# The closing feed-forward block of a cached decode kernel: seven batches moved beside the last tasks, the eighth handled alone

## The chip, the cores and the metric

The kernel runs on one core of a Trainium2 chip. The metric is device microseconds of one execution; the kernel before takes 1171.39 us (median of three runs, 1169.83 to 1171.56). Engines: PE (TensorE, matmuls, with PEld for its weight loads), DVE (VectorE), ACT (ScalarE), POOL (GpSimd), SP (SyncE, which here issues the DMAs).

## The reference

```
x = x + attn(layernorm(x), k_cache, v_cache, wq, wo)      # A
x = x + silu(layernorm(x) @ w1) @ w2                      # B
x = x + attn(layernorm(x), k_cache, v_cache, wq, wo)      # A again, same caches
x = x + silu(layernorm(x) @ w1) @ w2                      # B again
```

`x` is 8 batches x 1 token x 512. `attn` has 32 query heads over 8 KV groups of 8192 keys with 128 elements each, softmax over the keys, and no new key or value. The caches are 8 x 8 x 8192 x 128, bfloat16, K and V. w1 is 512 x 1792, w2 1792 x 512. The layer norm is (x - mean) / sqrt(var + 1e-5), without weights.

## The kernel before, in words

**Tasks.** One task is one (layer, batch, KV group); there are 128, in an order that `make_tasks` makes so that part of the K cache (20 of the 32 granules of a batch: groups 3 to 7) stays in SBUF between layer 0 and layer 1 of a batch. The last eight tasks are batch 7 in layer 1: groups 3 to 7 with kept K (tasks 120 to 124, only V is loaded), then groups 0 to 2 (tasks 125 to 127, K and V loaded). A task is eight positions `p` of the main loop, 1024 keys each.

**Loads.** `ARENA` is 28 slots of 512 KB. `plan_loads` fixes ahead which load goes to which slot, and after which position it may be issued (`after`); SP issues them in that fixed order (`issue_until`, `dma`, L428). Slot 8 is the home of group 3's first kept granule; from task 120 on it is free for other loads.

**One position.** At `p` PE transposes the K block of p + 1 (L523), DVE or ACT evicts it (L531, L529); on odd p PE makes the scores of two blocks (L562); on even p PE does P times V for the two blocks 12 positions back (L628). Between lie the softmax steps of the task before, at fixed phases of p: maximum (L573 to L577), shift (L581, L583), exponential (L587), sum (L593, L595), transposes of P (L603, L607), reciprocal (L614). `emit_norm` (L645) scales a finished head group into `QA`. All engines run their instructions in program order, so a piece that one of them waits for holds back what stands behind it on that engine.

**Pieces beside the tasks.** The end of a layer of a batch is cut in pieces; the main loop emits at most one or two of them per position: for layer 0 `chain_of` (wo, residual, layer norm, w1, Silu, w2, and the next queries, the `asks`). For layer 1, `heads[8]` collects the finished groups of batch 7, and `add_heads(8)` adds, for all eight batches at once, one group's part of the wo product to the PSUM bank `MISC` (`wo_part`, L743, 16 matmuls with 8 columns). The last of these comes after the last task.

**The closing block** (`closing`, L767 to L784) follows when all tasks are done, for eight batches together: residual (L755), layer norm in two passes (`normed`: sum over partitions on POOL, L670 and L672, center L676, square L700, second sum), w1 meanwhile (56 matmuls, L724, each column repeated four times, `AGAIN`), six filler matmuls (`keep_busy(AFTER)`, L543), the inverse root by a seed and three Newton rounds of three DVE instructions (`inverse_root`, L653 to L664), scaling on DVE (`scaled`, L706), Silu on ACT (L780), w2 (56 matmuls, L767) on top of the residual, a copy (L784) and four stores (L962).

Of the kernel before, what the change touches and what calls it, by code (L numbers as in the profile page):

```python
# [33 lines left out]
QSOON = 3  # L34
ASKS = (2, 5)
# [10 lines left out]
AGAIN = 4  # L46
BEFORE, AFTER = 4, 6
# [148 lines left out]
def plan_loads(tasks, kept, nslot, ngran):  # L196

    at = {t: i for i, t in enumerate(tasks)}
    homes = make_homes(kept, nslot, ngran)
# [89 lines left out]
def _build(ctx, nc, A_x, A_k_cache, A_v_cache, A_wq, A_wo, B_w1, B_w2, out):  # L289
# [99 lines left out]
    hsB = PTb[:, 0:FT * B]  # L389
    hB = Pf[:, 0:FT * B]  # L390
    ehB = Pf[:, FT * B:2 * FT * B]
    assert 5 * KT * B <= CPB * NQ * USED and FT * B <= 4 * KT * B and 4 * FT * B <= KB
# [49 lines left out]

    k_slot = {}
# [12 lines left out]
    with nc.Block() as block:  # L456

        @block.sync
        def _(sync_eng):
# [231 lines left out]
            def normed(xv, rx, w_sb, rw, outs, again=1):  # L691

                total(xv, rx, B)
                center(xbB, ["PT", "xb"], xv, rx, B)
                for f in project(w_sb, rw, outs, KT, lambda k: xbB[:, k, :], "xb", B, again=again):
                    f()
                if again > 1:
                    keep_busy(AFTER)
# [6 lines left out]
            def scaled(dst, rdst, n, again=1):  # L705
                op(dve, lambda: dve.tensor_tensor(  # L706
                    dst, MISC[:, 0:n * B * again].rearrange("p (h b) -> p h b", b=B * again)[:, :, 0:B],
                    yr[:, 0:B].unsqueeze(1).to_broadcast([128, n, B]), ALU.mult),
                   reads=["MISC", "yr"], writes=rdst)

            def project(w_sb, rw, outs, kparts, rhs_of, r_rhs, n, parts=1, again=1):

                steps = []
                w = CW if n == 1 else n * again

                def moved(k):
                    if n == 1:
                        return rhs_of(k).to_broadcast([128, w])
                    return rhs_of(k).unsqueeze(1).to_broadcast([128, again, n]) if again > 1 else rhs_of(k)

                for i, o in enumerate(outs):
                    for k in range(kparts):
                        steps.append(
                            lambda i=i, o=o, k=k: pe.matmul(  # L724
                                MISC[:, i * n:i * n + w] if again == 1 else
                                MISC[:, i * w:(i + 1) * w].rearrange("p (r b) -> p r b", b=n),
                                w_sb[:, k, o * 128:(o + 1) * 128], moved(k),
# [33 lines left out]
            def closing(x0, x1, r0, r1):  # L761

                rows = SCp[0]

                def quads(lhs_of, rhs_of, parts, first, last):
                    return [
                        lambda k=k, c=c: pe.matmul(  # L767
                            rows[c * QUAD:c * QUAD + B, 0:128], lhs_of(k, c), rhs_of(k, c),
                            start=first, stop=last and k == parts - 1,
                        )  # L770
                        for k in range(parts) for c in range(KT)
                    ]
# [7 lines left out]
                op(act, lambda: act.activation(hsB, hB, ACT.Silu), reads=["P"], writes=["hsB"])  # L780
# [83 lines left out]
            def add_heads(b):  # L864
# [6 lines left out]
                else:  # L871
                    wo_part(g, lambda h: QAv[:, h, :], every, B, first, last)
# [17 lines left out]
            scaled(QAv, every, HQ)  # L890
# [10 lines left out]
            ntask = len(tasks)  # L901

            for p in range(NG + LP + GPT + 1):
# [49 lines left out]
            assert not queue and not chain and not asks  # L953
# [39 lines left out]
```

## Time and profile before

| | us |
|---|---|
| median of three runs | 1171.39 (1169.83 to 1171.56) |
| the profiled execution | 1173.08 |
| its span | 1171.3 |
| PE busy / DVE / ACT / POOL over the span | 967.9 / 598.1 / 383.0 / 117.6 |
| DMA moved | 467.97 MB, mean 400 GB/s |
| last matmul of wo ends | 1162.3 |
| Silu of the closing block starts | 1167.37 |
| first store issued | 1169.05 |

The profile is of one execution. Times in the trace are microseconds from the start of its span; the execution's own time is 1.8 us longer than the span. "Busy" of PE is that of pipelined matmuls, so it overstates how much of PE is used. A name such as L523 is the line of the kernel that issues the instruction; "a<-b" says which tile is written from which.

### The profile page before, as it was taken

The page shows a single profiled execution, that of the slowest core. Times are in us where ns is not written, and L with a number is a line of the kernel's source. Part 1 is how long each engine was busy: PE and PEld are TensorE (multiplying, and loading weights), DVE is VectorE, ACT ScalarE, POOL GpSimd, SP SyncE. Part 2 cuts the span into 40 slices and gives each one's busy share as a digit, 9 for nine tenths or more (in the row PEclk, how much of TensorE's full clock was granted, in tenths as well). Part 3 has the DMA queues.
Part 4 walks back from the last instruction along what each step waited for, and adds up shares of the span by engine and source line. Part 5 has one row for each costly group of instructions (what it writes and reads, how often), then busy time and mean ns, then how long its engine had stood idle before and what let it go on. Part 6 is the DMA issues. An engine that isn't in the chain of part 4 may idle for free.

```text
span 1171.3 us, 44902 instructions
## 1 busy us (share of the span) xinstructions
PE 967.9 (83%) x19896; PEld 755.5 (65%) x19898; DVE 598.1 (51%) x1932; ACT 383.0 (33%) x660; POOL 117.6 (10%) x300
## 2 busy tenths in 40 slices
PE   4479888898889887888778887899878888788887
PEld 4367765677657675667557765677556666676665
DVE  2235654455545563556544563556445654556544
ACT  1124331343223331343223431334224332343222
POOL 0000111000100111001110111001100111001110
PEclk8789999899989999999998999999999999999999
DMA  9999999999999999999999999999999999999995
GB/s 346 394 398 389 402 408 417 422 397 382 411 423 412 366 409 416 423 395 405 411 423 376 401 408 419 421 383 409 413 421 414 385 408 421 409 387 407 411 411 227
DMA packets 96529, 467.97 MB, mean 400 GB/s; under 512 B 10056, under 2 KB 15952, under 8 KB 72784
## 3 DMA queue, kind: packets, MB, share of 16 engines
q1 hardware_dynamic: 96304, 465.10, 98.7%
q8 instruction: 157, 2.57, 0.9%
q14 instruction: 36, 0.29, 0.1%
q10 hardware_dynamic: 32, 0.00, 0.0%
HBM read 465.05 MB, written 0.01 MB: 397 GB/s over the span
## 4 chain that ended last, share of the span: by engine, by line
DMA 56%; PE 32%; DVE 5%; issue 4%; ACT 2%; SPq 1%; POOL 1%; POOLq 0%; ACTq 0%; DVEq 0%
DMA arena<-in_A_v_cache_dram 29%; DMA arena<-in_A_k_cache_dram 27%; PE TPp L523 11%; PE OTp L628 8%; PE SCp L562 6%; PE MISC L724 3%; ACT P L587 2%; PE TPp L603 2%; DVE arena L531 2%; DVE small L573 2%; PE MISC L743 1%; SPq L428 1%; POOL small L577 1%; DVE small L575 0%; DVE PT L607 0%
## 5 line engine op out<-in xcount | busy, mean ns | idle before, releaser
L523 PE MATMUL TPp<-ident,arena 128*128 128x128 bf16 x5632 | 447.3, 224 | 85.2 <-DMA arena<-in_A_k_cache_dram 82.3
L531 DVE COPY arena<-TPp 128x1024 bf16<-128x1024 bf16 x440 | 303.8, 690 | 327.0 <-PE TPp L523 325.2
L523 PEld LDWEIGHTS TPp<-ident,arena 128*128 128x128 bf16 x5632 | 333.4, 100 | 151.3 <-DMA arena<-in_A_k_cache_dram 99.0
L628 PE MATMUL OTp<-PT,arena 128*128 128x64 bf16 (+1 forms) x8192 | 318.9, 191 | 62.5 <-DMA arena<-in_A_v_cache_dram 39.0
L529 ACT COPY arena<-TPp 128x1024 bf16<-128x1024 bf16 x264 | 266.9, 1011 | 311.3 <-PE TPp L523 311.1
L628 PEld LDWEIGHTS OTp<-PT,arena 128*128 128x128 bf16 x8192 | 274.2, 98 | 104.8 <-DMA arena<-in_A_v_cache_dram 55.5
L562 PE MATMUL SCp<-arena,QB 128*32 128x512 bf16 x2048 | 208.9, 398 | 9.0 <-DVE small L614 4.3
L587 ACT ACTIVATE P<-SCp,small 128x512 bf16<-128x512 f32 x128 | 87.9, 687 | 391.6 <-DVE small L583 204.1
L577 POOL PARTITION_ALL_REDUCE small<-small x128 | 47.5, 371 | 720.4 <-DVE small L575 691.2
L573 DVE TENSOR_REDUCE small<-SCp 128x1 f32<-128x512 f32 x128 | 87.6, 684 | 40.2 <-PE SCp L562 39.2
L562 PEld LDWEIGHTS SCp<-arena,QB 128*32 128x32 bf16 x2048 | 54.0, 93 | 56.1 <-ACT QB L554 6.1
L595 POOL PARTITION_ALL_REDUCE small<-small x128 | 55.9, 436 | 240.7 <-DVE small L593 240.7
L607 DVE COPY PT<-TPp 128x256 bf16<-128x256 bf16 x128 | 37.3, 292 | 74.6 <-PE TPp L603 74.6
L603 PE MATMUL TPp<-ident,P 128*128 128x128 bf16 x512 | 51.2, 223 | 24.9 <-ACT P L587 24.9
L603 PEld LDWEIGHTS TPp<-ident,P 128*128 128x128 bf16 x512 | 29.1, 98 | 57.6 <-ACT P L587 47.0
L593 DVE TENSOR_SCALAR small<-small 128x4 f32<-128x4 f32 x128 | 29.2, 228 | 31.2 <-ACT P L587 29.9
L724 PE MATMUL MISC<-XT,wq 128*128 128x32 bf16 x1024 | 39.8, 177 | 1.5 <-issue 1.5
L724 PEld LDWEIGHTS MISC<-XT,wq 128*128 128x128 bf16 x1024 | 32.2, 96 | 9.0 <-issue 9.0
L743 PE MATMUL MISC<-at,wo 128*128 128x32 bf16 x1024 | 36.0, 176 | 1.4 <-issue 1.4
L743 PEld LDWEIGHTS MISC<-at,wo 128*128 128x128 bf16 x1024 | 31.6, 96 | 5.0 <-issue 5.0
L575 DVE SCALAR_TENSOR_TENSOR small<-small 128x4 f32<-128x4 f32 x128 | 28.5, 223 | 4.5
L581 DVE SCALAR_TENSOR_TENSOR small<-small 128x4 f32<-128x4 f32 x128 | 19.9, 156 | 20.4 <-POOL small L577 20.4
(69 smaller groups left out, 320.1 us busy)
## 6 DMA issues: line engine op xcount, KB each, us to landing
arena<-in_A_v_cache_dram SPq DMA_DIRECT2D x132, 1024.0 KB, 11.3
arena<-in_A_v_cache_dram SPq DMA_DIRECT2D x248, 512.0 KB, 8.0
arena<-in_A_k_cache_dram SPq DMA_DIRECT2D x192, 512.0 KB, 8.0
arena<-in_A_k_cache_dram SPq DMA_DIRECT2D x32, 2048.0 KB, 14.3
arena<-in_A_k_cache_dram SPq DMA_DIRECT2D x16, 1024.0 KB, 11.7
wq<-in_A_wq_dram SPq DMA_DIRECT2D x1, 4096.0 KB, 17.0
wo<-in_A_wo_dram SPq DMA_DIRECT2D x1, 4096.0 KB, 30.1
w<-in_B_w_dram SPq DMA_DIRECT2D x2, 1792.0 KB, 24.9
```

Source lines behind the costliest of these rows:

```text
L523: lambda c=c: pe.transpose(tpv[:, c, :], chunk(slot, h * GRP + c), ident[:, :])
L529: op(act, lambda: act.copy(dst, TPp[tb][:, :]), reads=[f"TP{tb}"], writes=[r_half(slot, h)])
L531: op(dve, lambda: dve.tensor_copy(dst, TPp[tb][:, :]), reads=[f"TP{tb}"], writes=[r_half(slot, h)])
L562: lambda c=c: pe.matmul(SCp[bank][c * QUAD:(c + 1) * QUAD, :], QB[qn][:, NGRAN - 1 - k:NGRAN - 1 - k + QUAD], ARENA[:, slot * SLOT + c * K ...
L573: op(dve, lambda: dve.tensor_reduce(rowmax, SCp[bank][:, :], AX.X, ALU.max), reads=[f"SC{bank}"], writes=["rowmax"])
L577: op(pool, lambda: pool.partition_all_reduce(tops, top, 128, bass.bass_isa.ReduceOp.max), reads=["top"], writes=["tops"])
L587: op(act, lambda: act.activation(P[:, :], SCp[bank][:, :], ACT.Exp, bias=shift, scale=SM_SCALE, accum_out=rs[st]), reads=[f"SC{bank}", "sh ...
L595: op(pool, lambda: pool.partition_all_reduce(ssa[st], ssm[st], 128, bass.bass_isa.ReduceOp.add), reads=[f"ssm{st}"], writes=[f"ssa{st}"])
L603: lambda c=c: pe.transpose(tpv[:, c, :], P[:, c * 128:(c + 1) * 128], ident[:, :])
L628: lambda c=c, cc=cc: pe.matmul(otp, chunk(slot, h * GRP + c), pv[:, cc % CPB, cc // CPB % NQ, k, :].unsqueeze(2).to_broadcast([128, REP, w ...
L724: lambda i=i, o=o, k=k: pe.matmul(MISC[:, i * n:i * n + w] if again == 1 else MISC[:, i * w:(i + 1) * w].rearrange("p (r b) -> p r b", b=n ...
L743: lambda o=o, h=h: pe.matmul(MISC[:, o * w:(o + 1) * w], wo_sb[:, h, o * 128:(o + 1) * 128], rhs_of(h).to_broadcast([128, w]) if n == 1 el ...
```

## The change

The closing block is split. Batches 0 to 6 are closed by `close_rest`, 18 pieces that the main loop emits from p = 979, when the last of their tasks is done: the first four on every odd position (`CLOSES` of the others wait), the other 14 one per position from p = 1000, the start of task 125. They work in slot 8, which the planner now keeps free from task 120 on. Their Silu is made of Exp, an addition, a reciprocal and a product. Batch 7 alone adds its heads to `MISC` afterwards, from p = 1014 on (one column, repeated 32 times), and `close_last` follows the last task: sums of x and of x squared come out of two DVE instructions and go through POOL together; the shift by the mean is on ACT; w1 and w2 work with one column; variance and inverse root are 12 DVE instructions, with Newton rounds of two; Silu reads `MISC` and has the inverse root as its scale. The filler matmuls are two before w1 and one behind it. The four stores become eight: seven rows each early, one row each at the end.

```
+CLOSES = 14
...
-AGAIN = 4
-BEFORE, AFTER = 4, 6
+BEFORE, BETWEEN, AFTER = 4, 2, 1
...
+    closes = at[(1, nb - 1, min(homes))]
+    spare = homes[min(homes)][1]
...
+                if d.task >= closes and slot <= spare < slot + n:
+                    continue
...
+    NR = B - 1
+    spare = make_homes(kept, NSLOT, NGRAN)[first][1]
+    SPf = ARENA[:, spare * SLOT:(spare + 1) * SLOT].bitcast(FP32)
...
-            def project(w_sb, rw, outs, kparts, rhs_of, r_rhs, n, parts=1, again=1):
+            def project(w_sb, rw, outs, kparts, rhs_of, r_rhs, n, parts=1):
...
+            def close_rest():
+                n = NR
+                x0, x1 = XT[2][:, :, 0:n], XT[1][:, :, 0:n]
+                hw = hR.rearrange("p (f b) -> p f b", b=n)
+
+                def second():
+                    center(xbR, ["xbR"] + spare_free, x1, "XT1", n)
+                    center(xcR, ["xcR"], x1, "XT1", n)
+                    op(dve, lambda: dve.tensor_tensor(sqR, xcR, xcR, ALU.mult), reads=["xcR"], writes=["sqR"])
+                    total(sqR, "sqR", n)
+
+                def expo():
+                    scaled(hw, ["hR"], FT, n)
+                    op(act, lambda: act.activation(ehR, hR, ACT.Exp, scale=-1.0), reads=["hR"], writes=["ehR"])
+
+                def silu():
+                    op(dve, lambda: dve.tensor_scalar(ehR, ehR, 1.0, None, op0=ALU.add), reads=["ehR"], writes=["ehR"])
+                    op(dve, lambda: dve.reciprocal(ehR, ehR), reads=["ehR"], writes=["ehR"])
+                    op(dve, lambda: dve.tensor_tensor(hsR, hR, ehR, ALU.mult), reads=["hR", "ehR"], writes=["hsR"])
+
+                def rows():
+                    tb = evacs[0] % NTP
+                    evacs[0] += 1
+                    bank = TPp[tb].bitcast(FP32)
+                    mm_group(
+                        quads(bank, n, lambda k, c: x1[:, c, :], lambda k, c: ident[:, :], 1, True, False)
+                        + quads(bank, n, lambda k, c: hsR[:, k * n:(k + 1) * n],
+                                lambda k, c: w2_sb[:, k, c * 128:(c + 1) * 128], FT, False, True),
+                        reads=["XT1", "ident", "hsR", "w2"], writes=[f"TP{tb}"])
+                    op(dve, lambda: dve.tensor_copy(outR, bank[:, 0:128]), reads=[f"TP{tb}"], writes=["outR"])
+
+                st = [lambda g=g: wo_part(g, lambda h: QAv[:, h, 0:n], every, n, g == 0, g == HKV - 1) for g in range(HKV)]
+                st = joined(st, lambda: add_residual(x1, "XT1", x0, "XT2", n, n))
+                st += [lambda: total(x1, "XT1", n), second]
+                w1 = project(w1_sb, "w1", range(FT), KT, lambda k: xbR[:, k, :], "xbR", n, 1 + NEWTON)
+                st += beside(w1, inverse_root(n))
+                return st + [expo, silu, rows, lambda: store(outR, "outR", 0, n, (sp,))]
+
+            def close_last():
+
+                x0, x1 = XT[2][:, :, NR:B], XT[1][:, :, NR:B]
                 rows = SCp[0]
-
-                def quads(lhs_of, rhs_of, parts, first, last):
-                    return [
-                        lambda k=k, c=c: pe.matmul(
-                            rows[c * QUAD:c * QUAD + B, 0:128], lhs_of(k, c), rhs_of(k, c),
-                            start=first, stop=last and k == parts - 1,
-                        )
-                        for k in range(parts) for c in range(KT)
-                    ]
+                a, z, y, t, v = sums, both, y1, t1, v1
+
+                def dv(f, reads, writes):
+                    op(dve, f, reads=reads, writes=writes)
 
                 op(act, lambda: act.activation(raw[:, 0:1], raw[:, 0:1], ACT.Silu), reads=["raw"], writes=["raw"])
-                add_residual(x1, r1, x0, r0, B, B)
-                mm_group(quads(lambda k, c: x1[:, c, :], lambda k, c: ident[:, :], 1, True, False),
-                         reads=[r1, "ident"], writes=["SC0"])
-                normed(x1, r1, w1_sb, "w1", range(FT), AGAIN)
-                scaled(hB.rearrange("p (f b) -> p f b", b=B), ["P"], FT, AGAIN)
-                op(act, lambda: act.activation(hsB, hB, ACT.Silu), reads=["P"], writes=["hsB"])
-                mm_group(quads(lambda k, c: hsB[:, k * B:(k + 1) * B], lambda k, c: w2_sb[:, k, c * 128:(c + 1) * 128],
+                dv(lambda: dve.scalar_tensor_tensor(
+                    x1[:, :, 0], MISC[:, 0:KT * CW].rearrange("p (k b) -> p k b", b=CW)[:, :, 0], 1.0, x0[:, :, 0],
+                    op0=ALU.mult, op1=ALU.add, accum_out=a[:, 0:1]), ["MISC", "XT2"], ["XT1", "sums"])
+                dv(lambda: dve.scalar_tensor_tensor(
+                    sq1b, x1[:, :, 0], 1.0, x1[:, :, 0], op0=ALU.mult, op1=ALU.mult, accum_out=a[:, 1:2]),
+                   ["XT1", "sums"], ["sums", "sq1b"])
+                op(pool, lambda: pool.partition_all_reduce(both, sums, 128, bass.bass_isa.ReduceOp.add),
+                   reads=["sums"], writes=["both"])
+                mm_group(quads(rows, 1, lambda k, c: x1[:, c, :], lambda k, c: ident[:, :], 1, True, False),
+                         reads=["XT1", "ident"], writes=["SC0"])
+                keep_busy(BETWEEN)
+                op(act, lambda: act.activation(off1, z[:, 0:1], ACT.Copy, scale=-1.0 / D), reads=["both"], writes=["off1"])
+                op(act, lambda: act.activation(xb1, x1[:, :, 0], ACT.Identity, bias=off1), reads=["XT1", "off1"], writes=["xb1"])
+                project(w1_sb, "w1", range(FT), KT, lambda k: xb1[:, k:k + 1], "xb1", 1)[0]()
+                keep_busy(AFTER)
+                dv(lambda: dve.tensor_scalar(m1, z[:, 0:1], z[:, 0:1], 1.0 / D / D, op0=ALU.mult, op1=ALU.mult),
+                   ["both"], ["m1"])
+                dv(lambda: dve.scalar_tensor_tensor(u1, z[:, 1:2], 1.0 / D, m1, op0=ALU.mult, op1=ALU.subtract),
+                   ["both", "m1"], ["u1"])
+                dv(lambda: dve.tensor_scalar(v, u1, 0.0, LN_EPS, op0=ALU.max, op1=ALU.add), ["u1"], ["v1"])
+                dv(lambda: dve.tensor_scalar(u1, v, -0.5, None, op0=ALU.mult), ["v1"], ["u1"])
+                yi, vi = y.bitcast(INT32), v.bitcast(INT32)
+                dv(lambda: dve.tensor_scalar(yi, vi, 1, None, op0=ALU.logical_shift_right), ["v1"], ["y1"])
+                dv(lambda: dve.tensor_scalar(yi, yi, -1.0, RSQRT_SEED, op0=ALU.mult, op1=ALU.add), ["y1"], ["y1"])
+                for _n in range(NEWTON):
+                    dv(lambda: dve.tensor_scalar(t, y, y, u1, op0=ALU.mult, op1=ALU.mult), ["y1", "u1"], ["t1"])
+                    dv(lambda: dve.scalar_tensor_tensor(y, t, 1.5, y, op0=ALU.add, op1=ALU.mult), ["t1", "y1"], ["y1"])
+                op(act, lambda: act.activation(hs7, MISC[:, 0:FT], ACT.Silu, scale=y), reads=["MISC", "y1"], writes=["hs7"])
+                mm_group(quads(rows, 1, lambda k, c: hs7[:, k:k + 1], lambda k, c: w2_sb[:, k, c * 128:(c + 1) * 128],
                                FT, False, True),
-                         reads=["hsB", "w2"], writes=["SC0"])
-                op(dve, lambda: dve.tensor_copy(P[:, 0:128], rows[:, 0:128]), reads=["SC0"], writes=["P"])
+                         reads=["hs7", "w2"], writes=["SC0"])
+                dv(lambda: dve.tensor_copy(out1, rows[:, 0:128]), ["SC0"], ["out1"])
+                store(out1, "out1", NR, 1, (sp, act))
 
...
-                    wo_part(g, lambda h: QAv[:, h, :], every, B, first, last)
+                    wo_part(g, lambda h: QAv[:, h, NR:B], every, 1, first, last)
...
+            rest = None
+            ended = [0]
+            streamed = task_at[(1, B - 1, 0)] * GPT
...
+                elif rest is None and not asks and turn[0] == B and ended[0] == NR * HKV:
+                    rest = close_rest()
+                    rest.pop(0)()
+                elif rest and (p >= streamed or len(rest) > CLOSES and p % GPG == GPG - 1):
+                    rest.pop(0)()
                 elif not setup and not asks and heads[turn[0]] and (p >= NG or turn[0] == B
                                          or p % GPG == GPG - 1 and (tasks[p // GPT][2], 0) in kept):
-                    add_heads(turn[0])
+                    if turn[0] < B or rest == []:
+                        add_heads(turn[0])
...
+                    else:
+                        ended[0] += 1
...
-            closing(XT[2][:, :, :], XT[1][:, :, :], "XT2", "XT1")
-            for eng in (sp, act):
-                syn.acquire(eng, reads=[res("P")])
-            for c in range(KT):
-                (sp, act)[c % 2].dma_start(
-                    out_v[:, c * 128:(c + 1) * 128], P[c * QUAD:c * QUAD + B, 0:128]).then_inc(osem, 16)
-            sp.wait_ge(osem, 16 * KT)
+            close_last()
+            sp.wait_ge(osem, 2 * 16 * KT)
 
 
 # ---- launch: one core; inputs and outputs as the reference has them ----
```

`quads` and `store` (new) are the row matmuls and the stores of before as helpers with the number of rows as an argument; `normed`, `scaled` and `project` lose the argument `again`, and `total`, `center` and `inverse_root` are called with seven columns.

More of the change, by code (lines that the diff above doesn't have):

```diff
@@ L198, in plan_loads @@
     at = {t: i for i, t in enumerate(tasks)}
+    nb = 1 + max(b for _l, b, _g in tasks)
     homes = make_homes(kept, nslot, ngran)
@@ L388, in _build, with spared @@
     xbB = PTb[:, 4 * KT * B:5 * KT * B].rearrange("p (k b) -> p k b", b=B)
[L389 to L392, printed above, removed]
+    NR = B - 1
+    spare = make_homes(kept, NSLOT, NGRAN)[first][1]
+    SPf = ARENA[:, spare * SLOT:(spare + 1) * SLOT].bitcast(FP32)
+    gone = [0]
+    def spared(n, dt=FP32):
+        w = -(-n * mybir.dt.size(dt) // 4)
+        v = SPf[:, gone[0]:gone[0] + w]
+        gone[0] += w
+        return v if dt == FP32 else v.bitcast(dt)[:, 0:n]
+    xcR, sqR = [spared(KT * NR).rearrange("p (k b) -> p k b", b=NR) for _ in range(2)]
+    xbR = spared(KT * NR, BF16).rearrange("p (k b) -> p k b", b=NR)
+    hR, ehR = [spared(FT * NR) for _ in range(2)]
+    hsR, outR = spared(FT * NR, BF16), spared(128, BF16)
+    xb1, sq1b = spared(KT, BF16), spared(KT)
+    sums, both = spared(2), spared(2)
+    v1, m1, u1, y1, t1 = [spared(1) for _ in range(5)]
+    off1 = spared(1)
+    hs7 = spared(FT, BF16)
+    out1 = spared(128, BF16)
+    assert gone[0] <= SLOT // 2 and 5 * KT * B <= CPB * NQ * USED
     SCp = [ps_bank("SCp") for _ in range(NSCP)]
@@ L441, in _build @@
     out_v = out.rearrange("b s d -> (b s) d")
+    spare_free = [r_half(spare, h) for h in range(GPG)]
     k_slot = {}
@@ L689, in ln_stages, with normed @@
                 return [lambda: total(xv, rx, 1), second] + inverse_root(1)
-            def normed(xv, rx, w_sb, rw, outs, again=1):
+            def normed(xv, rx, w_sb, rw, outs):
                 total(xv, rx, B)
                 center(xbB, ["PT", "xb"], xv, rx, B)
-                for f in project(w_sb, rw, outs, KT, lambda k: xbB[:, k, :], "xb", B, again=again):
+                for f in project(w_sb, rw, outs, KT, lambda k: xbB[:, k, :], "xb", B):
                     f()
-                if again > 1:
-                    keep_busy(AFTER)
                 center(xcB, ["xcB"], xv, rx, B)
@@ L703, in normed, with scaled @@
                     f()
-            def scaled(dst, rdst, n, again=1):
+            def scaled(dst, rdst, n, b):
                 op(dve, lambda: dve.tensor_tensor(
-                    dst, MISC[:, 0:n * B * again].rearrange("p (h b) -> p h b", b=B * again)[:, :, 0:B],
-                    yr[:, 0:B].unsqueeze(1).to_broadcast([128, n, B]), ALU.mult),
+                    dst, MISC[:, 0:n * b].rearrange("p (h b) -> p h b", b=b),
+                    yr[:, 0:b].unsqueeze(1).to_broadcast([128, n, b]), ALU.mult),
                    reads=["MISC", "yr"], writes=rdst)
-            def project(w_sb, rw, outs, kparts, rhs_of, r_rhs, n, parts=1, again=1):
+            def project(w_sb, rw, outs, kparts, rhs_of, r_rhs, n, parts=1):
                 steps = []
[L714 to L719, printed above, removed]
+                w = CW if n == 1 else n
                 for i, o in enumerate(outs):
@@ L724, in project @@
                             lambda i=i, o=o, k=k: pe.matmul(
-                                MISC[:, i * n:i * n + w] if again == 1 else
-                                MISC[:, i * w:(i + 1) * w].rearrange("p (r b) -> p r b", b=n),
-                                w_sb[:, k, o * 128:(o + 1) * 128], moved(k),
+                                MISC[:, i * n:i * n + w], w_sb[:, k, o * 128:(o + 1) * 128],
+                                rhs_of(k).to_broadcast([128, w]) if n == 1 else rhs_of(k),
                                 start=(k == 0), stop=(k == kparts - 1),
@@ L759, in add_residual @@
                 )
-            def closing(x0, x1, r0, r1):
-                rows = SCp[0]
-                def quads(lhs_of, rhs_of, parts, first, last):
-                    return [
-                        lambda k=k, c=c: pe.matmul(
-                            rows[c * QUAD:c * QUAD + B, 0:128], lhs_of(k, c), rhs_of(k, c),
-                            start=first, stop=last and k == parts - 1,
-                        )
-                        for k in range(parts) for c in range(KT)
-                    ]
-                op(act, lambda: act.activation(raw[:, 0:1], raw[:, 0:1], ACT.Silu), reads=["raw"], writes=["raw"])
-                add_residual(x1, r1, x0, r0, B, B)
-                mm_group(quads(lambda k, c: x1[:, c, :], lambda k, c: ident[:, :], 1, True, False),
-                         reads=[r1, "ident"], writes=["SC0"])
-                normed(x1, r1, w1_sb, "w1", range(FT), AGAIN)
-                scaled(hB.rearrange("p (f b) -> p f b", b=B), ["P"], FT, AGAIN)
-                op(act, lambda: act.activation(hsB, hB, ACT.Silu), reads=["P"], writes=["hsB"])
-                mm_group(quads(lambda k, c: hsB[:, k * B:(k + 1) * B], lambda k, c: w2_sb[:, k, c * 128:(c + 1) * 128],
@@ new lines, in quads, with store @@
+            def quads(rows, n, lhs_of, rhs_of, parts, first, last):
+                return [
+                    lambda k=k, c=c: pe.matmul(
+                        rows[c * QUAD:c * QUAD + n, 0:128], lhs_of(k, c), rhs_of(k, c),
+                        start=first, stop=last and k == parts - 1,
+                    )
+                    for k in range(parts) for c in range(KT)
+                ]
+            def store(src, rsrc, lo, n, engines):
+                for eng in set(engines):
+                    syn.acquire(eng, reads=[res(rsrc)])
+                for c in range(KT):
+                    engines[c % len(engines)].dma_start(
+                        out_v[lo:lo + n, c * 128:(c + 1) * 128], src[c * QUAD:c * QUAD + n, 0:128]).then_inc(osem, 16)
@@ L889, in _ @@
             normed(XT[0][:, :, :], "XT0", wq_sb, "wq", range(HQ))
-            scaled(QAv, every, HQ)
+            scaled(QAv, every, HQ, B)
             emit_q(0)
@@ L952, in _ @@
                 issue_until(p)
-            assert not queue and not chain and not asks
+            assert not queue and not chain and not asks and rest == []
             while heads[B]:
```

## The prediction

> **What bounds the kernel now.** I read the windows first. Until 1155 the cache loads keep the DMA engines full; PE has room beside them.
>
> ```profile
> 1140.00:1150.00 10.00, 8.45 (x173) 6.73 (x170) 5.68 (x16) 4.42 (x8) 1.04 (x3) 1.00 1.03 408
> 1150.00:1155.00 5.00, 4.53 (x100) 3.52 (x99) 1.89 (x5) 2.02 (x2) 0.19 (x1) 1.00 1.03 407
> 1155.00:1160.00 5.00, 3.85 (x99) 2.89 (x97) 1.86 (x8) 2.27 (x4) 0.80 (x2) 1.00 0.66 260
> ```
>
> The columns are the stretch and its length, then PE, weight loads, DVE, ACT and POOL busy, granted clock, DMA share, GB/s. DMA share is 1.03 up to 1155, with PE at 84 to 91%. Next the chain that ended last, in order of time:
>
> ```profile
> 1145.25 15.56 DMA arena<-in_A_v_cache_dram
> ...
> 1161.69 0.60 PE MISC L743 x16
> ...
> 1162.84 0.42 POOL small L672
> ...
> 1164.08 0.47 POOLq L456
> ...
> 1166.79 0.18 DVE small L664
> ...
> 1167.06 0.29 DVE P L706
> 1167.37 0.31 ACT PT L780
> 1167.72 0.98 PE SCp L767 x56
> ```
>
> The end is the landing of the last V piece, at 1160.8, and behind it a serial tail: PV, norm, wo (done at 1162.29, "t0" below), layer norm, Silu, w2, store, end at 1171.3. DMA is left as it is, so only the tail after t0 can shrink; 9.0 us are there. Third, PE's timeline, because the change puts work on PE ahead of t0:
>
> ```profile
> 1146.93 0.62 PE L523 MATMUL TPp<-ident,arena 128*128 128x128 bf16 x8 [0.66 <-DMA arena<-in_A_k_cache_dram]
> 1149.49 0.62 PE L523 MATMUL TPp<-ident,arena 128*128 128x128 bf16 x8 [0.65 <-DMA arena<-in_A_k_cache_dram]
> ...
> 1154.42 0.40 PE L562 MATMUL SCp<-arena,QB 128*32 128x512 bf16 x4 [0.47 <-DVE small L614]
> ...
> 1158.45 0.96 PE L628 MATMUL OTp<-PT,arena 128*128 128x48 bf16 x32
> ...
> 1160.86 0.57 PE L628 MATMUL OTp<-PT,arena 128*128 128x48 bf16 x16 [0.66 <-DMA arena<-in_A_v_cache_dram]
> ```
>
> PE waits for K pieces, and at the end for V; but the last score group (1154.42) leads through the softmax to the last PV only from 1158.45.
>
> **Part 1, the tail of the last batch.** Before, Silu on ACT starts at 1167.37 (t0+5.08) and w2 at 1167.72 (t0+5.43). After, step by step:
> - Residual with its sum: 0.02 + 0.17 (L755 at 128x4), x1 at t0+0.20. Square with its sum: 0.02 + 0.17, t0+0.39. No row shows DVE's accumulator output: between nothing and a separate reduce (L670, 0.16 + 0.02) each. I take nothing, as other DVE rows here cost the same 0.15 to 0.17 whatever they do.
> - POOL: 0.08 + 0.41 (L672): both sums at t0+0.88.
> - On ACT: 0.04 + 0.20 (L774, 128x1), 0.03 + 0.27 for the shift with a bias operand (0.20 plus some 0.07; no row on 128x4 has one), t0+1.42. Then PE: 0.05 + 1.67 (w1, 56 matmuls, row 1163.53): done at t0+3.14. BETWEEN's two matmuls (0.27 each at full clock, 0.43 at half) lie in PE's wait from t0+0.5 to t0+1.47.
> - On DVE, beside it: 12 instructions. Four have a per-partition scalar operand, and that costs 0.07, as two groups of one shape show:
>
> ```profile
> L575 DVE SCALAR_TENSOR_TENSOR small<-small 128x4 f32<-128x4 f32 x128 | 28.5, 223 | 4.5
> L581 DVE SCALAR_TENSOR_TENSOR small<-small 128x4 f32<-128x4 f32 x128 | 19.9, 156 | 20.4 <-POOL small L577 20.4
> ```
>
>   m1 0.23, five at 0.155, three Newton rounds at 0.23 + 0.16, 11 gaps of 0.027: 2.47; from t0+0.91 to t0+3.38. Two scalars in one instruction may cost 0.07 more, three times. The rounds are shorter in count (6 for 9), hardly in time: the 12 instructions of before take 2.42 (1164.57 to 1166.99).
> - Silu from PSUM at t0+3.41, 0.28 (L827's 0.215 on 128x14 plus 0.07): w2 at t0+3.74 instead of t0+5.43. Gain 1.69; with both unknowns against it 1.1. **I take 1.6.** It comes from the second pass (center, square, reduce, POOL: 1163.28 to 1164.57) and the scaling (0.38), not from Newton. w2, the copy and four store issues have the same counts; I give them nothing (eight rows to one row per store: 0 to 0.2).
>
> PE's cover is thin: w1 is done 0.25 before Newton. If w1 started 0.3 later, it would be the bound.
>
> **Part 2, batches 0 to 6 beside the tasks.** All 18 pieces run at positions p = 979 to 1013: four wo pieces in the kept tasks (979, 981, 983, 985), the rest one per p from 1000 (from p = 1000, at 1126.3, to p = 1013, at 1142.2). Batch 7's own eight wo pieces, one per task before, are held back to 1014 to 1019, 1027 and 1035.
> - Kept tasks: there the softmax loop sets the pace (5.5 per task, with wo's 0.41 in it). Two of that loop's wo pieces go (987, 995), one comes in (981), two lie in PE's 1.2 wait before L603. p = 1000 comes some 0.4 sooner, and waits at once for a K piece (1127.96). Worth nothing.
> - Added to PE up to the last score group: four wo pieces (16 matmuls, 0.43), w1 in four parts (14 x 0.0285 = 0.40), the rows (60 x 0.0175 = 1.05), and five wo pieces at 1014 to 1018; gone are those at 1003 and 1011. Net 5.5. Going through the positions with PE's start-to-start times and the landing times as floors: up to p = 1009 the added 2.5 lies in waits for data (0.6 at 1127.96, 0.7 at 1133, 0.6 at 1136.8, 0.8 at 1138). From there to 1013: w1's last part 0.40, the rows 1.05, their wait for Silu behind DVE's queue 0.64, less 0.43 that goes: with 0.1 of stalls, 1.76 late. Then 2.15 of wo pieces against start-to-start waits of 0.4 (1144.37), 0.8 and 0.8: 1.9 late, and 0.2 of small stalls back: **the last score group is 1.65 late**.
> - What that costs: PV of the last task starts with PT's copy at 1158.4 and needs 64 x 0.0277 = 1.8 and 0.1, so without waits it would be done at 1160.3, where now it is 1161.45. So 1.15 is free, and 0.5 shows. DVE has 5.2 more work between p = 1003 and 1013 (12 small instructions at 0.2, five at 0.2 on up to 128x28, scaled and the three of Silu 1.2, a copy 0.3, residual 0.2), on 57% load over 12 us: nearly full. I add 0.2 for evictions that wait there. **t0 comes 0.7 later**; bounds: 0 (all late work is caught up) to 3.
> - Queues: SP's four stores at p = 1013 stand behind the last cache load (released at p = 1001, issued by 1147.1 because SP is held back by the queue). Nothing on SP is behind them until the end, so their wait costs nothing, nor do POOL's two extra reductions. Leaving one slot out of 28 free of late loads moves a few loads to slots freed within two positions; the 2.6 MB queued at 1126.4 (13.1 moved from there to 1158.5, less 10.5 still to issue) cover that, and cover a slower kept stage.
>
> **Sum.** 1173.08 (span 1171.3 and 1.8 around it) - 1.6 + 0.7 = 1172.2; that profiled run stands 1.69 above the median of the three shown, so 1171.39 - 0.9 = **1170.5**.
>
> **PE's clock.** Windows of half a microsecond show the granted clock at half for 3.4 us in this tail:
>
> ```profile
> 1162.50:1163.00 0.50, 0.23 (x4) 0.09 (x4) 0.21 (x2) 0.00 (x0) 0.16 (x1) 0.87 0.00 0
> ...
> 1166.50:1167.00 0.50, 0.50 (x3) 0.10 (x1) 0.39 (x3) 0.00 (x0) 0.00 (x0) 1.00 0.00 0
> ```
>
> It is back at 1166.3 (t0+4.0), before w2. After, w2 starts at t0+3.74 with three filler matmuls in the place of six. If half clock covers w2, its 14 rounds of four 128-column matmuls take 14 x 0.107 = 1.5 (the fillers go from 0.27 to 0.43 and more) in place of 0.98: +0.5. [...]
>
> **Rivals.**
> - *Forecast*, 0.40: 1170.5, own range 1169.7 to 1171.2.
> - *All of part 2 is covered* (DVE keeps up, PE absorbs it): -1.6 to -1.8, 1169.7. For: DMA waits of 4.6 between 1127 and 1150. Against: they lie ahead of the pieces at 1012 to 1018. 0.20.
> - *Half clock in w2*: 1170.5 + 0.5 = 1171.0. 0.20.
> - *PE and DVE back up* (slower): the rows at p = 1012 wait in PE's order for Silu, which waits in DVE's order behind Newton and evictions; every transpose and score behind them moves. Each us beyond 1.15 of lateness at the last score group is a us at the end. From 2.75 late the gain is gone; at 5.0 the time is 1171.39 - 1.6 + 3.85 = 1173.6, with half clock 1174.1. For: DVE nearly full. Against: only 5.2 of added work, most of it short. 0.15, spread over 1171.4 to 1174.
> - *A table load comes back on ACT* before the shift: 1.28 (ACT_TABLE_LOAD) later, w1 done at t0+4.4, gain 0.7, t0 0.7 later: 1171.4. Against: COPY and Exp share one table over the whole run. [...] 0.05.
>
> **Range and chances.** 0.2% is 2.34 us, about what a measurement of this kernel can tell from no change: below 1169.05 is faster, above 1173.73 slower. Three runs here lie 1.7 apart, so the covered case may measure below 1169.05. Range 1168.6 to 1173.0. Faster 0.18, same 0.72, slower 0.10.
>
> **What would show it.** Part 1: from the end of the last wo to the first w2 matmul 3.7 to 4.3, with one POOL reduction. Part 2: the last score group 1.65 later against the last V landing (1160.8 should stay), and the last PV without a wait for DMA. I am wrong if the loads land later, if DVE's accumulator outputs are separate instructions, or if w1 and not Newton ends last.

## The result: slower, 1176.9 us, and what the profile after shows

The kernel after takes 1176.94 us (median of 7 runs, 1173.75 to 1177.98) beside 1170.59 for the kernel before in the same comparison (7 runs); the ratio is 1.0046, with a 95% interval of 1.0031 to 1.0061. By this ratio it is slower by 5.4 us, outside the range of 1168.6 to 1173.0. Its profiled execution took 1177.98 us, with a span of 1175.7.

Of the 4.4 us by which the span grew, the tail has little. The last wo ends (t0, as in the prediction) at 1167.5 in place of 1162.3: 5.2 later. From there w2 starts at t0+3.92 in place of t0+5.43: 1.5 won. w2 itself ran at half clock in this execution (granted 0.50 from 1171.4 to 1173.1), 1.69 in place of 0.98: 0.7 lost. 5.2 - 1.5 + 0.7 = 4.4. These are times of one execution each. Here is the chain that ended last, of after:

```profile
1146.49 2.34 issue
...
1160.87 0.42 PE SCp L586 x4
...
1167.98 0.47 POOLq L480
...
1171.11 0.28 ACT arena L868
1171.44 1.69 PE SCp L779 x56
```

The tail from 1167.98 on is the one that the change means: one POOL reduction, twelve DVE instructions, Silu, w2. What was not forecast stands ahead of it. The last score group is at 1160.87, before at 1154.42: 6.45 later. And on the way there the chain has an entry of 2.34 with the name "issue": PE did nothing, and no wait that the profile knows ended it; such a pause is called a stop below. PE's timeline of after shows where the stops lie (the bracket is the idle time before the group, and what ended it):

```profile
1141.16 0.33 PE L547 MATMUL TPp<-ident,arena 128*128 128x128 bf16 x3 [1.06 <-issue]
1143.75 0.23 PE L779 MATMUL TPp<-ident,XT 128*7 128x128 bf16 x4 [0.56 <-DVE arena L811]
1148.83 0.26 PE L652 MATMUL OTp<-PT,arena 128*128 128x48 bf16 x4 [2.34 <-issue]
1160.87 0.40 PE L586 MATMUL SCp<-arena,QB 128*32 128x512 bf16 x4 [0.47 <-DVE small L638]
1164.91 1.77 PE L652 MATMUL OTp<-PT,arena 128*128 128x48 bf16 x64
```

These stops fall inside groups whose operands are all there: eight transposes of one K block are cut after five (1141.16), a PV group of 16 after 12 (1148.83). With 0.32 at 1128.59, 0.88 at 1134.80 and 0.32 at 1155.41 they add up to 4.92 us. Between two of them PE always runs 127 matmuls; with a weight load each, and two semaphore instructions that the trace has there, that makes 256. The last line answers to the last PV of before, which waited for V: now it runs 64 matmuls without a wait, so the data were there first. The windows of after say the same (columns as in the prediction):

```profile
1146.00:1148.00 2.00, 0.49 (x16) 0.41 (x14) 0.78 (x2) 0.46 (x2) 0.00 (x0) 1.00 1.03 404
1150.00:1152.00 2.00, 2.00 (x32) 1.37 (x30) 0.00 (x0) 1.01 (x1) 0.00 (x0) 0.50 1.04 416
1156.00:1158.00 2.00, 2.00 (x51) 1.67 (x48) 0.59 (x3) 1.01 (x1) 0.43 (x1) 1.00 0.18 70
```

In the first, PE works a quarter of the time while the DMA engines are full (1.03). In the second its clock is at half (0.50), after the long stop; the repeat of after below has the same stop (2.34), but behind it eight transposes take 0.61 (1145.06), where after's took 1.01 (1149.34), so the half clock isn't part of every execution. In the third the loads are done (0.18), where before they held a share of 0.66 up to 1160: the end is no longer the landing of V, but PE.

What is it that PE lacks? Among the page's DMA queues, after and before have one of its own for instructions:

```profile
q8 instruction: 158, 2.59, 0.9%
```

158 packets and 2.59 MB are 16 KB each; 40,278 matmuls and weight loads over 158 are 255. So by this count one packet brings the 256 instructions of one stretch. In the trace's DMA records of after these packets start at 1126.2, 1132.2, 1138.6, 1146.3 and 1152.8, take 1.0 to 1.1 us each, and PE goes on 2.4 to 2.6 us after each start (1128.59, 1134.80, 1141.16, 1148.83, 1155.41). The theory: **PE runs out of instructions**, because the next block is fetched through DMA engines that are full of cache loads. What it costs here are the 4.92 us of stops, in the 36.0 from p = 1000 to the last score group.

The trace of before shows it too, elsewhere, and it could have been read there. PE's timeline of before, at the end of batch 6:

```profile
1068.83 0.26 PE L628 MATMUL OTp<-PT,arena 128*128 128x48 bf16 x4 [0.98 <-issue]
1075.72 0.28 PE L724 MATMUL MISC<-XT,wq 128*128 128x32 bf16 x5 [1.29 <-issue]
1081.96 0.42 PE L628 MATMUL OTp<-PT,arena 128*128 128x48 bf16 x10 [0.32 <-issue]
```

Again 127 matmuls lie between each two. Over its whole span before has 12 stops of 0.3 us or more under "issue", 9.0 us in all. None lies behind 1082.

### The profile page after: what moved, and what is told of

It reads as the page before. It is cut to its first block, busy times and chain, and to the rows that moved or that the text cites. A ratio compares the mean times of both kernels' runs of the same rounds, so it can differ in the third digit from the quotient of the medians.

```text
span 1175.7 us, 45414 instructions
## 1 busy us (share of the span) xinstructions
PE 967.0 (82%) x20139; PEld 758.2 (64%) x20139; DVE 600.4 (51%) x1952; ACT 384.1 (33%) x663; POOL 118.2 (10%) x301
## 3 DMA queue, kind: packets, MB, share of 16 engines
q8 instruction: 158, 2.59, 0.9%
## 4 chain that ended last, share of the span: by engine, by line
DMA 56%; PE 32%; DVE 5%; issue 4%; ACT 2%; POOL 1%; SPq 0%; POOLq 0%; ACTq 0%
DMA arena<-in_A_k_cache_dram 29%; DMA arena<-in_A_v_cache_dram 26%; PE TPp L547 12%; PE OTp L652 9%; PE SCp L586 6%; PE MISC L741 3%; ACT P L611 2%; PE TPp L627 2%; PE MISC L759 2%; DVE small L597 1%; DVE arena L555 1%; POOL small L601 1%; DVE PT L631 0%; DVE small L599 0%; DVE small L607 0%
## 5 line engine op out<-in xcount | busy, mean ns | idle before, releaser
L617 DVE TENSOR_SCALAR small<-small 128x4 f32<-128x4 f32 x128 | 29.1, 228 | 29.8 <-ACT P L611 28.6
L741 PEld LDWEIGHTS MISC<-XT,wq 128*128 128x128 bf16 x1024 | 32.2, 96 | 8.8 <-issue 8.7
## 6 DMA issues: line engine op xcount, KB each, us to landing
wo<-in_A_wo_dram SPq DMA_DIRECT2D x1, 4096.0 KB, 30.2
```

What stands on the lines that cost most here:

```text
L741: lambda i=i, o=o, k=k: pe.matmul(MISC[:, i * n:i * n + w], w_sb[:, k, o * 128:(o + 1) * 128], rhs_of(k).to_broadcast([128, w]) if n == 1 ...
```

## The experiments

All twelve kernels stand beside before, with ratios and their 95% intervals (no_loads ran once and has none); "window" below is the time from the transposes of p = 1000 to the last score group. Two theories stood against each other first. **Fetch**: what counts is the number of PE instructions beside the cache loads. **Work**: what counts is the time of the added work on PE and DVE and its waits, as the prediction had it.

**Number against time.** To before, 19 groups of fillers are added on PE, once with 12 matmuls of 32 columns (228 more matmuls, as many as the change adds in the window), once with 3 of 256 columns (57 more, with twice the columns in all).

```
+                if 1000 <= p <= 1018:
+                    filler(12, 32)        # fill_narrow;  fill_wide: filler(3, 256)
```

> The kernel before with twelve extra matmuls of 32 columns (0.0285 us each, into an unused part of MISC) at each position from 1000 to 1018: 228 matmuls, 6.5 us of PE time, nothing else. Fetch theory (PE's instructions come in blocks of 256, that is 127 matmuls with their weight loads, and each block takes 6.2 to 7.7 us to arrive while the cache loads run): 492 + 228 = 720 matmuls from p = 1000 to the last score group, 5.7 blocks, so that group comes 6 to 8 us later than 1154.4 and the time is 5 to 7 us above before; PE stands still 0.3 to 2.4 us in the middle of groups, some 127 matmuls apart. Rival (PE's own time, as the prediction counted it): 6.5 us against 4.6 us of waits for data, last score group 2 to 2.5 late, 1 to 1.5 us above before.

> The same with three matmuls of 256 columns in the place of each twelve: 57 matmuls, about the same PE time (0.11 us each, 6.3 us), a quarter of the instructions. Fetch theory: 549 matmuls, 4.3 blocks, which fit in the 28 us that these positions take anyway: 0 to 1.5 us above before, far below the narrow ones. Rival (PE's own time): the same as the narrow ones, whatever that is.

Measured: fill_narrow 1176.12 beside 1170.96, ratio 1.0044 [1.0029, 1.0059]; fill_wide 1170.46 beside the same, 0.9996 [0.9981, 1.0011]. PE's timeline of fill_narrow, then of fill_wide:

```profile
1128.42 0.18 PE L905 MATMUL MISC<-wq,ident 128*128 128x32 bf16 x1 [0.84 <-issue]
1134.61 0.22 PE L628 MATMUL OTp<-PT,arena 128*128 128x64 bf16 x2 [0.93 <-issue]
1140.79 0.33 PE L905 MATMUL MISC<-wq,ident 128*128 128x32 bf16 x7 [1.06 <-issue]
...
1146.96 0.36 PE L628 MATMUL OTp<-PT,arena 128*128 128x48 bf16 x8 [1.02 <-issue]
...
1153.30 0.18 PE L628 MATMUL OTp<-PT,arena 128*128 128x48 bf16 x1 [1.34 <-issue]
...
1158.37 0.40 PE L562 MATMUL SCp<-arena,QB 128*32 128x512 bf16 x4 [0.47 <-DVE small L614]
```

```profile
1153.81 0.40 PE L562 MATMUL SCp<-arena,QB 128*32 128x512 bf16 x4 [0.47 <-DVE small L614]
```

The number of matmuls alone brings a loss of the size of after's, without any of its DVE work, waits or stores; the last score group is at 1158.37 with many small ones, and at 1153.81 with few wide ones. It came 4.0 later than in before, not the 6 to 8 expected, but p = 1000 was 2.5 sooner in this execution: the window is 6.5 longer. The stops end every 6.2 us (6.19, 6.18, 6.17, then 6.34): that is the pace of a block of 127 matmuls here, beside full DMA engines (share 1.02 to 1.03 in after from 1128.6 to 1141.2, where the stops end 6.21 and 6.36 apart). In after, its repeat and fill_narrow the five stops come at the same counts of PE's matmuls from the start of the trace (19,251, then 127 more each time), whatever matmul lies there. Before goes slower than that by itself, 484 matmuls in a window of 28.1, so 7.4 for 127.

**How it sets in.** Six and nine fillers per position in place of twelve.

```
+                    filler(6, 32)         # fill_half;  fill_most: filler(9, 32)
```

> Half the narrow fillers: six matmuls of 32 columns at each position from 1000 to 1018 in the kernel before, 114 in all, 3.2 us of PE time. Fetch theory: 606 matmuls are 4.8 blocks at 6.2 to 7.7 us, 30 to 33 us where before takes 28, less some 1.15 that is free at the end: 1 to 3 us above before, with two to four gaps in the middle of groups. Rival (PE's own time): 3.2 us lie within the 4.6 of waits: 0 to 0.5 us above before.

> Nine narrow fillers at each position from 1000 to 1018 in the kernel before, 171 in all, 4.9 us of PE time: 655 matmuls from p = 1000 to the last score group, between the half dose (598, in 28.4 us, time as before) and the full one (712, in 34.6 us, 5.2 above before). Fetch theory, with the block at 6.0 us as the half dose suggests: 655 / 127 x 6.0 = 31 us, 1 to 2 us above before, gaps of 1.5 to 3.5 in sum. Rival (PE's own time): 0 to 0.8 above before and no gaps.

fill_half: 1170.76 beside 1169.94, 1.0002 [0.9989, 1.0015]. fill_most: 1172.43 beside 1170.37, 1.0022 [1.0010, 1.0033]. Half the load was expected to cost 1 to 3 and costs nothing that can be told; fill_most was expected at 1 to 2 and costs 2.6 by the ratio. The loss doesn't grow evenly with the number: it sets in between 598 and 655 matmuls. In the windows:

| kernel | matmuls | window, us | stops in it, us | matmuls/127 x 6.2 |
|---|---|---|---|---|
| before | 484 | 28.1 | 0 | 23.6 |
| fill_wide | 541 | 29.8 | 0 | 26.4 |
| fill_half | 598 | 28.4 | 0.69 | 29.2 |
| fill_most | 655 | 32.2 | 3.68 | 32.0 |
| fill_narrow | 712 | 34.6 | 5.19 | 34.8 |
| after | 712 | 36.0 | 4.92 | 34.8 |

Up to 598 matmuls the window follows something else (PE's work and its waits for data), from 655 on 6.2 us per block. After lies 1.2 above, and one of its blocks took 7.7 in place of 6.2 (1141.16 to 1148.83).

**Is it the cache loads that make it slow?** After, with the loads of tasks 125 to 127 not issued; everything else on PE is the same.

```
-        dma(sp, dst, src, slsem[d.slot], ...)
+        if d.task < 125:
+            dma(sp, dst, src, slsem[d.slot], ...)
```

> The changed kernel without the K and V loads of the last three tasks (125 to 127 work on what lies in the slots; these loads are left out, PE, DVE and ACT issue all that they issued). Fetch theory (a block of instructions is late because it queues behind the cache loads): with the DMA engines idle from about 1135 on, a block takes 2.5 to 3 us, PE never stands still in the middle of a group by more than 0.3 us, and from p = 1000 to the last score group it takes 27 to 30 us in the place of 36. Rival (PE stands still for a reason of its own, whatever the DMA engines do): gaps of 0.3 to 2.3 us remain some 127 matmuls apart, and these positions take 33 us or more.

One execution, 1170.61 us. The windows of no_loads, and its last score group:

```profile
1130.00:1140.00 10.00, 9.35 (x224) 7.93 (x220) 7.63 (x32) 3.90 (x7) 1.60 (x4) 1.00 0.02 5
1140.00:1150.00 10.00, 9.36 (x269) 7.91 (x266) 5.88 (x16) 3.61 (x6) 0.80 (x2) 1.00 0.02 4
```

```profile
1155.01 0.40 PE L587 MATMUL SCp<-arena,QB 128*32 128x512 bf16 x4 [0.47 <-DVE small L639]
```

With a DMA share of 0.02 PE runs up to 269 matmuls in 10 us (4.7 per 127) and has no stop inside a group: here, with the DMA engines free, no block came late. The window is 29.7 with the same 712 matmuls and the same work on DVE. After itself waits for no load in its window (its waits there are the stops, 4.92, and 1.03 for DVE), so beside after the edit takes away the stops and the half clock, and no wait for data. Beside before it can't be read as the price of the added work: before waits 3.8 us for K and V in its window, and this kernel can't. That it comes out 1.6 longer than before's, near the prediction's 1.65, is luck.

**Part 1 without part 2.** After without the pieces of `close_rest`, so that only `close_last` is left of the change. The kernel leaves out the closing of batches 0 to 6 and stores zeros for their rows, and batch 7's wo pieces are back at their old places.

```
-            rest = None
+            rest = []
...
+                if p == 1013:
+                    op(dve, lambda: dve.memset(outR, 0.0), writes=["outR"] + spare_free)
+                    store(outR, "outR", 0, NR, (sp,))
```

> The changed kernel without the work of closing batches 0 to 6 (their rows are stored as zeros; this work is left out), batch 7's heads at their old places: the new tail alone. Both theories: PE's stream up to the last score group is that of before, so the last wo ends where it did before, 1.1 to 1.6 us are gained between there and the end with full clock in w2, 0.4 to 0.9 if w2 runs at half clock; time 0.4 to 1.6 us below before. Rival (the new tail is itself at fault): last wo as in before and the time at or above before.

1169.40 beside 1170.96, 0.9987 [0.9974, 1.0000]. The timeline of tail_alone from the last wo on:

```profile
1155.90 0.57 PE L759 MATMUL MISC<-QA,wo 128*128 128x32 bf16 x16 [0.26 <-DVE QA L669]
1156.59 0.09 DVE L841 DVE_READ_ACCUMULATOR XT<-MISC,XT 128x1 f32 x1
...
1156.99 0.41 POOL L847 PARTITION_ALL_REDUCE arena<-arena  x1 [4.47 <-DVE arena L844]
...
1158.50 0.27 DVE L866 TENSOR_SCALAR arena<-arena 128x1 f32<-128x1 f32 x1
...
1160.07 0.27 ACT L868 ACTIVATE arena<-MISC,arena 128x14 bf16<-128x14 f32 x1 [2.05 <-DVE arena L867]
1160.39 0.95 PE L779 MATMUL SCp<-w,arena 128*1 128x128 bf16 x56 [0.75 <-ACT arena L868]
```

With t0 at 1156.49, w2 starts at t0+3.90 and takes 0.95, as before's does at a granted 1.00. The new tail is worth 1.5 us of path, and the time falls by about that (1.5 by the ratio, with an interval that reaches from 3.0 to nothing).

**Part 2 taken apart.** In late, batch 7's wo pieces wait until p = 1024 and the last two pieces of the rest (rows, store) until the tasks are done; in heads_late only the wo pieces wait. Both leave out the four fillers that `keep_busy(BEFORE)` puts after the last task.

```
-                    if turn[0] < B or rest == []:
+                    if turn[0] < B:
                         add_heads(turn[0])
+                    elif p >= NG:
...
```

> The changed kernel with batch 7's heads held back to p = 1024 and later (two at 1024 and 1025, then one at 1027 and from 1029), the rows and the store of batches 0 to 6 at p = 1031 and 1033, and without the four filler matmuls at 1027. Fetch theory: 140 matmuls fewer ahead of the last score group, 4.6 blocks in the place of 5.7: that group 4 to 6 us earlier than in the changed kernel; the pieces then lie in PE's waits for the softmax and the last V. Time 1 us below to 2 us above before. Rival (PE's own time, DVE's queue): the work ahead of the last wo is the same, so at most 1 to 2 us below the changed kernel, 3 to 5 above before.

> The changed kernel with only batch 7's heads held back to p = 1024 and later (and without the four fillers at 1027); rows and store of batches 0 to 6 stay at p = 1012 and 1013. 632 matmuls from p = 1000 to the last score group in the place of 712. Fetch theory: 632 / 127 x 6.0 to 6.3 = 30 to 31.5 us in the place of 36; time 2 to 4 us below the changed kernel, 1 to 3 above before, so most of the loss hangs on these 80 matmuls. Rival (the rows' wait for Silu is the loss): the wait of 0.6 at the rows remains, and the time stays within 1 us of the changed kernel.

late: 1172.13 beside 1170.96, 1.0015 [1.0001, 1.0029], 556 matmuls in a window of 30.2. heads_late: 1173.81 beside 1170.37, 1.0033 [1.0015, 1.0050], 616 in 32.2. The fewer matmuls stay beside the loads, the less is lost: by the ratios +5.4 for after, +3.9 for heads_late, +1.8 for late. heads_late was expected at 1 to 3 above before and came out above that. Both keep one long stop, here that of late:

```profile
1142.57 0.33 PE L547 MATMUL TPp<-ident,arena 128*128 128x128 bf16 x3 [2.11 <-issue]
```

It makes all of late's 2.1 of window, though 556 matmuls need only 27.1 by the pace of 6.2. After, its repeat and heads_late have such a stop of 2.34, fill_narrow has none over 1.34. The four stores of the rest are issued near it in three of these kernels (in after from 1145.22), but in late 20 us behind it (1163.4), so they aren't its cause. The five blocks of after show where the long one lost its time. From the 38th matmul of a block to the first of the next, each took 4.4 to 5.1 us, the long one 5.1; its first 37 took 2.6, those of the others 1.3 to 2.2, and PE's wait for Silu (0.56 at 1143.75) lies among them. That would fit a next block that is asked for some 37 matmuls into a block, so that a wait of PE ahead of that point delays it too; but in late these two parts are 5.8 and 1.6, so the cause stays open.

**Fewer instructions for the rows.** In rows_wide (of after) the product of Silu with w2 for batches 0 to 6 is made of 14 matmuls with 512 columns in place of 56 with 128, and one store in place of four; after_again is after, unchanged, on the same chip.

```
-                        + quads(bank, n, ..., FT, False, True),
+                        + [lambda k=k: pe.matmul(bank[0:n, 0:D], hsR[:, k * n:(k + 1) * n], w2_sb[:, k, 0:D], ...)
+                           for k in range(FT)],
```

> The changed kernel with the rows of batches 0 to 6 made by 14 matmuls of 512 columns in the place of 56 of 128 (four at a time), and one store in the place of four: 42 matmuls fewer, at least 2 us more PE time (14 x 0.22 = 3.1 against 1.0), DVE's copy 0.4 us longer. Fetch theory: 42 matmuls are a third of a block, 1.5 to 2.5 us less waiting; the last score group 0 to 2 us earlier than in the changed kernel, time 0 to 2 us below it. Rival (PE's own time): last score group 2 us later, time 2 us above the changed kernel.

> The changed kernel unchanged, as the yardstick for the runs beside it on this chip: 4 to 7 us above before by every theory.

rows_wide 1175.54, after_again 1175.36, both beside 1170.72: 1.0043 [1.0028, 1.0059] and 1.0050 [1.0032, 1.0068]. The group of rows in rows_wide:

```profile
1144.11 3.18 PE L820 MATMUL TPp<-w,arena 128*7 128x512 bf16 x14
```

Half a miss: stops fell to 3.01 (6.39 in after_again) and the window to 35.0 (36.2), but these 14 matmuls take 3.18 of PE where the 60 small ones took about 1.0, and the time can't be told from that of after.

**Part 1 in the old closing block.** Before, with all eight batches in the closing block, but x and x squared summed in one POOL pass, two Newton rounds, and six fillers (onepass) or two (onepass_few) behind w1. Nothing is moved beside the tasks.

```
-                normed(x1, r1, w1_sb, "w1", range(FT), AGAIN)
+                op(dve, lambda: dve.tensor_reduce(s2[:, 0:B], x1.rearrange("p k b -> p b k"), AX.X, ALU.add), ...)
+                op(dve, lambda: dve.tensor_tensor(sqB, x1, x1, ALU.mult), ...)
+                op(dve, lambda: dve.tensor_reduce(s2[:, B:2 * B], sqB.rearrange("p k b -> p b k"), AX.X, ALU.add), ...)
+                op(pool, lambda: pool.partition_all_reduce(s2a, s2, 128, bass.bass_isa.ReduceOp.add), ...)
...
+                for f in inverse_root(B)[:-1]:
+                    f()
...
-BEFORE, AFTER = 4, 6
+BEFORE, AFTER = 4, 2                      # onepass_few alone
```

> The kernel before, all eight batches in the closing block, with the sums of x and x squared in one POOL reduction and two Newton rounds: no work is moved beside the tasks. Fetch theory: PE's stream up to the last wo is that of before, so only the tail changes: one POOL pass, a center and three DVE instructions less against two more DVE instructions, 0.7 to 1.0 us shorter from the last wo to the end, time 0.5 to 1.2 us below before. Rival (the shorter tail is not worth anything, as something else sets the end): no change in the tail.

> The kernel before with one POOL reduction and two Newton rounds for all eight batches, and two filler matmuls behind w1 in the place of six (with six, the fillers at half clock ended last and held w2 back to 5.3 us behind the last wo). Theory (the tail's DVE steps are what w2 waits for once the fillers are few): w2 starts 4.5 to 4.8 us behind the last wo in the place of 5.4; with full clock in w2 0.6 to 0.9 us below before, with half clock 0 to 0.3. Rival (the fillers are needed for the clock): w2 takes 1.5 to 1.7 and nothing is left of the gain.

onepass: 1171.04 beside 1170.72, 1.0004 [0.9991, 1.0018]. onepass_few: 1170.18 beside 1169.94, 1.0002 [0.9989, 1.0015]. Fillers and w2 on PE, of onepass, then of onepass_few:

```profile
1161.84 1.76 PE L543 MATMUL TPp<-wq,ident 128*128 128x512 bf16 x5 [0.22 <-issue]
1163.53 0.95 PE L767 MATMUL SCp<-w,PT 128*8 128x128 bf16 x56
```

```profile
1165.90 0.63 PE L543 MATMUL TPp<-wq,ident 128*128 128x512 bf16 x1 [0.22 <-issue]
1166.80 1.67 PE L767 MATMUL SCp<-w,PT 128*8 128x128 bf16 x56 [0.27 <-ACT PT L799]
```

In onepass Silu was done at 1162.70, but the fillers, five in 1.76 us, ended last and held w2 to t0+5.25; by that time most of them ran at half clock (in before they start 0.42 to 0.43 apart at a granted 0.50, and 0.21 to 0.23 at 1.00). With two fillers w2 starts at t0+4.46, and in this execution runs at half clock itself by its time, 1.67 in place of 0.95 (after's took 1.66 at a granted 0.50): what the shorter chain wins, the clock takes here. That it is so in the other executions, whose median time is that of before, isn't shown. No kernel that does the whole computation beat before.

## Why the prediction was wrong, step by step

- **The step that failed** is part 2, "the last score group is 1.65 late", and with it "t0 comes 0.7 later". PE was counted by the time of its matmuls and its waits for data alone; the arrival of its instructions stands in the sum at nothing, without a reason. Whether the rest of the sum was right can't be told: no run has the added work, the loads and no stops. (Its parts add up to 5.7 us of PE time, not 5.5.) Beside the loads 712 matmuls need 5.6 blocks of instructions at 6.2 us, 34.8, where before took 28.1; fill_narrow, which adds only the number, loses 5.2 by its ratio. The group was 6.45 late, and t0 5.2.
- "1.15 is free" and "each us beyond 1.15 is a us at the end" held: 6.45 - 1.15 = 5.3, measured 5.2. These are two executions; by windows it comes to the same. After's is 7.8 longer (36.2 in the repeat: 8.1), 1.2 of that comes back between the last score group and t0, and the span from t0 to the end is 0.9 shorter (1.6 in the repeat, with w2 in 0.95): 5.7 and 5.3, beside 5.4 and 5.9 by the ratios.
- "p = 1000 comes some 0.4 sooner" can't be told: 1124.91 for 1126.30 here, but 1120.36 in the repeat of after, and 1121.0 in onepass, whose code up to there is before's.
- The slower rival, "PE and DVE back up", had the right sign, its 0.15 was too little, and its mechanism isn't needed for the loss: the rows' wait for Silu is there (0.56 at 1143.75, 0.64 assumed), but fill_narrow, which has nothing of it, loses as much. At most it has a part in the one long block.
- Queues: the loads didn't starve; the DMA engines were done before PE (share 0.18 at 1156 to 1158). Their last large packets end at 1158.3, in before at 1160.4. That "with PE at 84 to 91%" there was room beside full DMA engines was half a reading of the windows: the 57 wide matmuls of fill_wide did fit, the 228 narrow ones of fill_narrow did not. Busy time did not tell how soon the next instructions come (a stop of 0.84 to 1.34 us every 6.2 in fill_narrow). The row for it was in before's timeline at 1068.83 to 1081.96, under "issue".
- **Part 1** was right within its bounds: w2 at t0+3.90 and t0+3.92 (3.74 forecast), so 1.5 won (1.6 taken). Of its unknowns, two scalar operands in one instruction cost 0.27 (L866) in place of 0.23, three times, a little less than feared. The accumulator output is a separate instruction, which the prediction had named as a sign of being wrong, but it takes 0.09 and lies within the time of the one before.
- "Half clock in w2" came in one profile of after (1.66 in the timeline) and not in the other (1167.09, 0.95), and cost 0.7, not 0.5. Of the seven profiles with the new tail two have it, after and rows_wide (its last stores start some 6.0 us behind the last wo, as after's do; those of the repeat 5.2). No run shows what decides whether the clock is halved there; these two profiles of one kernel differ in it.
- "A table load comes back" is refuted: the shift follows its predecessor on ACT with 0.09 between (1168.47 + 0.20, then 1168.76), no load between; the trace's two loads of 1.28 lie at 5.3 and 1164.0.

Left open: why one block in kernels with the changed closing takes some 7.7 us (7.4 in late), and how far ahead of PE a block is asked for. No run tests these.

## What to carry to other kernels

Work that was put beside the cache loads of this kernel (DMA share 1.02 to 1.03) had two prices on PE: its time (14 wide matmuls for the rows took 3.18 us, 60 small ones 1.01) and its number of instructions (228 narrow fillers cost 5.2 us, 57 wide ones with twice the columns nothing that can be told). Look in the trace of the kernel as it is for idle time under "issue" inside a matmul group, at equal numbers of matmuls. The time between two neighbouring stops tells what work moved there must reckon with; here it was about 6.2 us for 127 matmuls, with 5.6 to 7.7 over all the traces, so it is a yardstick and not a fixed rate. Work of many small matmuls goes where the loads are done, or is made of fewer ones, as long as these don't take longer themselves.

## What the runs showed of the hardware beside that

- While cache loads filled the DMA engines (share 1.02 to 1.03 in after from 1128.6 to 1141.2), PE went through one stretch of 256 instructions in 6.2 to 6.4 us, its stop included; while they were idle (0.02 in no_loads), through one in 4.7 (269 matmuls in 10 us, without a stop).
- A PE stop of 2.34 us was followed by half clock for 3.4 us (1149.3 to 1152.7) in after, and in its repeat by matmuls that took as long as at full clock (eight transposes 0.61, against 1.01).
- Filler matmuls became the path in onepass: five of 512 columns took 1.76 us and ended last.
- 14 matmuls of 512 columns and 7 rows took 3.18 us in rows_wide, 0.23 each; 60 of 128 columns, which four at a time write to different rows of the bank, took 1.01 in after (1143.75), 0.017 each.
